# Load order, holds, banks and blank products at the start of a retention and ELU kernel

## The chip, the cores and the metric

The kernel runs on one core of a Trainium2 chip. The metric is the device time of one execution in microseconds (us), of which several runs are made and the median is given. A separate execution is recorded by the hardware profiler, and all lines of profile in this document come from such executions. The engines are TensorE (PE: matrix products, PEld: loading of their stationary operand), VectorE (DVE), ScalarE (ACT), GpSimd (POOL) and SyncE (SP), which here issues every transfer between HBM and SBUF.

## The reference

A retention layer (a linear attention with a decaying state, per head) is followed by a feed-forward layer with an ELU. All values are fp32.

```python
B, H, S, D = 4, 8, 768, 64                       # q, k, v: (B, H, S, D)
gamma = 1.0 - 2.0 ** (-5.0 - np.arange(H))
for t in range(S):
    state = gamma * state + k[:, :, t] (outer) v[:, :, t]
    y[:, :, t] = q[:, :, t] @ state / np.sqrt(D)
x = y.transpose(0, 2, 1, 3).reshape(3072, 512)
h = x @ w_in                                      # 512 x 2048
g = np.where(h > 0.0, h, np.exp(np.minimum(h, 0.0)) - 1.0)
out = g @ w_out                                   # 2048 x 512
```

## The kernel before

The 3072 tokens are handled in six blocks of 512 tokens, and a block in four chunks of 128. For each chunk two tiles of 0.5 MB are loaded: `qk` (q and k, transposed) and `kvn` (k and v). The retention of a chunk is computed in 64-token halves. `score_products` makes the scores (L276, 64x64 products into `sc`), `mask_pair` or `scores` masks them on VectorE (L297, L287), `scale_v` multiplies v by the decay (L250, or L247 on ACT for chunk 3), `state_products` and `state_sum` make the states (L307; L317, L319), and `outputs` makes the outputs `y` from scores (L341) and from states (L367), with a tiny copy `seen` (L355) between two groups of accumulations. At its end `outputs` multiplies `y` by the decay table `etab` into the block's input `xb` (L376). Before the first output exists, tables are set up: positions by POOL, `etab` by four exponentials on ACT (L209), `vf` for the scaling of v, and the mask `cmask`.

The weights arrive as 16 pieces of 1 MB of float64 bits (`wraw`, through a ring of three `stage` buffers). A piece is turned into fp32 by two steps on ACT (`prepare`, L142 and L144) and four on VectorE (`decode`, L165, L168, L171, L174); when a piece has been decoded, the next one is loaded into its buffer. Pieces 0 to 7 are `w_a` and `w_b` (from `w_in`), pieces 8 to 15 become `w_s` (from `w_out`).

The first block is computed plainly: `plain_first` (L443 for the first five tiles of hidden units, in two token halves, then L454) and `plain_second` (L468). While it runs, combinations of the weights are made by VectorE (`combine_w_out`, L509; `combine_w_in`, L536) and stored to scratch memory. From the second block on the products use Strassen's scheme: `first` (L602), later `first_twice` and `second_twice` (L772, L811), which fetch the stored combinations (`wq`).

The order of the instructions on each engine is the order in which the program writes them; no scheduler changes it. At the start `prepare(2)` and `take(4)` decode the first half of piece 0, and then chunks 0 and 1 are worked through. `take()` advances the decoding of the current piece by one VectorE step. The loads stand in front of everything:

```python
    load_piece()
    load(0)
    load(1)
    load_piece()
    load(2)
    load(3)
    load_piece()
```

PSUM is divided into a ring of four banks (`ps_r`: scores, states, outputs and some hidden tiles) and four fixed banks: `a` (two buffers), `b` and `d`.

Of the kernel before, what the change touches and what calls it, by code (L numbers as in the profile page):

```python
# [9 lines left out]
FP32 = mybir.dt.float32  # L10
# [7 lines left out]
def kernel(  # L18
# [32 lines left out]
    nc = tc.nc  # L51
# [45 lines left out]
    def load(m):  # L97

        if m >= NCHUNK:
            return  # L100
        qk = ldpool.tile([P, 2, HP, C], FP32, name="qk", tag="qk")
        nc.sync.dma_start(qk.rearrange("p a h c -> p (a h c)"), qkv[m, :, 0:1024])
        kv = ldpool.tile([C, 2, H, D], FP32, name="kvn", tag="kvn")
        nc.sync.dma_start(kv.rearrange("p a h c -> p (a h c)"), qkv[m, :, 1024:2048])
        raw[m] = (qk, kv)

# [4 lines left out]
    NPIECE = 2 * NQ + NF  # L113
    staged, prepared, decoded = [], [], []

    def load_piece():
        n = len(staged)
        if n < NPIECE:

            t = stage.tile([P, 1024, 2], U32, name="wraw", tag="stage")  # L120
            nc.sync.dma_start(t.rearrange("p c w -> p (c w)"), w_bits[n].bitcast(U32))
            staged.append(t)

# [57 lines left out]
        for _ in decode():  # L181
            pass

    load_piece()
    load(0)
    load(1)
    load_piece()
    load(2)
    load(3)
    load_piece()  # L190


    pos_t = t4.tile([P, S], I32, name="pos_t", tag="t4")
    nc.gpsimd.iota(pos_t, pattern=[[1, S]], base=0, channel_multiplier=0)


    head = lambda a, u, c: 2 * (2 * u + c) + a
# [1 line left out]
    for a in range(2):  # L199
        for u in range(2):  # L200
            for c in range(2):
                nc.vector.memset(lny[c * D : (c + 1) * D, a, u : u + 1], math.log(gammas[head(a, u, c)]))

    post = t4.tile([P, S], FP32, name="post", tag="t4")
    nc.vector.tensor_copy(post, pos_t)
    etab = const.tile([P, 2, 2, S], FP32, name="etab")
    for a in range(2):
        for u in range(2):
            nc.scalar.activation(etab[:, a, u, :], post, AF.Exp, scale=lny[:, a, u : u + 1])  # L209
    pos_s = const.tile([P, NCH, H], I32, name="pos_s")  # L210
    nc.gpsimd.iota(pos_s, pattern=[[C, NCH], [0, H]], base=0, channel_multiplier=1)
    lng = const.tile([P, H], FP32, name="lng")
    for h in range(H):
        nc.vector.memset(lng[:, h : h + 1], math.log(gammas[h]))
# [13 lines left out]
    for sub in range(2):  # L228
        r = slice(sub * D, (sub + 1) * D)
        nc.vector.tensor_copy(cmask[r, :], causal[r, r])  # L230

    xb = const.tile([P, 4, TB], FP32, name="xb")
# [5 lines left out]
    def scale_v(m):  # L240
        if m >= NCHUNK:
            return
        i = chunks[m][1]
        qk, kv = raw[m]
        if m == 3:
            for h in range(H):
                nc.scalar.activation(kv[:, 1, h, :], kv[:, 1, h, :], AF.Copy, scale=vf[:, i, h : h + 1])  # L247
            return
        eng = nc.vector if m == 0 else nc.gpsimd
        eng.tensor_tensor(  # L250
            out=kv[:, 1], in0=kv[:, 1], in1=vf[:, i].unsqueeze(2).to_broadcast([C, H, D]), op=ALU.mult
        )
# [76 lines left out]

    def outputs(tb, pp, first=False):  # L330

        y = [ps_r.tile([P, 2 * 2, 2, D], FP32, name="y", tag="r") for _ in range(2)]
        for x in range(2):
            kv = raw[tb * CPB + 2 * pp + x][1]
            for j in range(4):
                a, u = divmod(j, 2)
                pt = raw[tb * CPB + 2 * pp + (x if first else a)][0][:, 1].rearrange("p h c -> p (h c)")
                for sub in range(2):
                    for c in range(2):
                        p = 2 * u + c  # L340
                        nc.tensor.matmul(  # L341
                            y[sub][rows(c), j, x, :], lhsT=kv[rows(sub), 1, head(a, u, c), :],
                            rhs=pt[rows(sub), ((a if first else x) * HP + p) * D :][:, 0:D],
                            start=(x == 0 and j == 0), stop=False, skip_group_check=True,
                        )
            if first and x == 0:
                yield
        for other in range(2):
            if not other:
                yield  # L350
            else:

                for sub in range(2):
                    seen = epool.tile([P, 8], FP32, name="seen", tag="seen")
                    nc.vector.tensor_copy(seen.rearrange("p (j x) -> p j x", x=2), y[sub][:, :, :, 0])  # L355
                yield
            for x in range(2):
                q = raw[tb * CPB + 2 * pp + x][0]
                for u in range(2):
                    for a in range(2):  # L360
                        sub = a ^ other
                        n = 4 * pp + 2 * x + sub
                        if fresh(tb, n):
                            continue
                        for c in range(2):
                            p = 2 * u + c
                            nc.tensor.matmul(  # L367
                                y[sub][rows(c), 2 * a + u, x, :], lhsT=state(tb, n)[rows(a), p, :],
                                rhs=q[rows(a), 0, p, rows(sub)], start=False, stop=True, skip_group_check=True,
                            )  # L370
        if first:
            yield
        i = chunks[tb * CPB + 2 * pp][1]
        for sub in range(2):
            place = lambda t: t.rearrange("p j (x s c) -> p j x s c", x=2, s=2)[:, :, :, sub, :]
            nc.vector.tensor_tensor(  # L376
                out=place(xb[:, :, 2 * pp * C : 2 * (pp + 1) * C]), in0=y[sub],
                in1=place(etab.rearrange("p a u t -> p (a u) t")[:, :, i * C : (i + 2) * C]), op=ALU.mult,
            )
# [81 lines left out]
    def plain_second():  # L461

        ops = [bank(x).rearrange("p a b -> p (a b)") for x in "aabd"]
        for n, f in enumerate(ORDER_F):
            wo = decoded[2 * NQ + n]
            for row in range(2):
                for d in range(4):
                    nc.tensor.matmul(  # L468
                        ops[d], lhsT=wo[:, row, (d if row else d ^ 2) * P :][:, 0:P], rhs=g_plain[row * NF + f],
                        start=(n == 0 and row == 0), stop=(n == NF - 1 and row == 1),  # L470
                    )
            so = t4.tile([P, 4, 256], FP32, name="so", tag="t4")
            tt = lambda o, x, y, op: nc.vector.tensor_tensor(out=o, in0=x, in1=y, op=op)
            a21, a11, a12, a22 = (wo[:, r, 256 * d : 256 * d + 256] for r in range(2) for d in range(2))
            tt(so[:, 0], a21, a22, ALU.add)
            tt(so[:, 1], so[:, 0], a11, ALU.subtract)
            tt(so[:, 2], a11, a21, ALU.subtract)
            tt(so[:, 3], a12, so[:, 1], ALU.subtract)
            nc.sync.dma_start(quarters(f)[:, 8:16], so.rearrange("p a (d c) -> p (a d) c", c=P))
            if n < 5:  # L480
                send_small()
            sources = wo.rearrange("p r (d c) -> p (r d) c", d=2)[:, 1:4], so
            if n % 2:
                last = combine_w_out(n // 2, low, sources)

                for _ in itertools.islice(last, 8 if n < NF - 1 else 4):
                    pass
            low = sources
            if n >= 5:
                send_small()  # L490
            held["last"] = last if n % 2 else None
            yield
        for d in range(4):
            ot = gq["T3"][:, 2 * d : 2 * d + 2, :]
            eng = (nc.scalar.copy, nc.vector.tensor_copy)[d % 2]
            eng(ot.rearrange("p a b -> p (a b)"), ops[d])
            nc.sync.dma_start(out[0, d // 2, :, :, d % 2, :].rearrange("t p c -> p t c"), ot)
# [453 lines left out]
    def take(count=1):  # L951
        for _ in range(count):
            next(piece, None)

    prepare(2)
    piece = decode(True)
    take(4)
    sc = [ps_r.tile([P, 2, HP, D], FP32, name="sc", tag="r") for _ in range(2)]
    score_products(sc, 0, 0, 0)
    scale_v(0)  # L960
    scale_v(1)
    mask_pair(sc, 0)
    kvs = [ps_r.tile([P, 2, HP, D], FP32, name="kv", tag="r") for _ in range(2)]
    state_products(kvs, 0, 0, 0, range(2))
    score_products(sc, 0, 0, 1)
    state_sum(kvs, 0, 0, 0, 0)
    state_sum(kvs, 0, 0, 0, 1)
    mask_pair(sc, 1)
    take(2)
    prepare()  # L970
    y = outputs(0, 0, True)
    next(y)
    state_products(kvs, 0, 0, 1, [0])
    next(y)
    state_sum(kvs, 0, 0, 1, 0)
    take()

    next(y)
    next(y)
    state_products(kvs, 0, 0, 1, [1])  # L980
    take(2)
    next(y, None)
    state_sum(kvs, 0, 0, 1, 1)
    scale_v(2)
    decode_all()
# [251 lines left out]
```

## Time and profile before

| | |
|---|---|
| runs before | 646.38, 647.08, 647.72, 648.02 us; median 647.39 us |
| profiled execution | 646.38 us, of which the recorded span is 644.6 us |
| TensorE busy | 629.8 us, 98% of the span |
| VectorE busy | 496.5 us, 77% |
| ACT busy | 240.4 us, 37% |
| POOL busy | 39.3 us, 6% |
| moved by transfers | 139.72 MB, 217 GB/s on average |
| first product on TensorE | 7.50 us after the span's start |
| first product of `plain_first` | 19.03 us |

A row of a timeline gives the start, the length, the engine, the line, the operation and its tiles. A row of the chain of waits gives the start, the length and the work that the end was waiting for at that time. An entry of the waits reads: engine, line and tile, what it waited for, the sum in us, how many times, and the longest. Transfers are listed by line with their size and the time from issue to landing.

### The profile page before, as it was taken

The numbers are of one execution on the slowest core, as the hardware profiler recorded it, in microseconds if no ns is written. First come the engines' busy times: TensorE is split into PE (matmuls) and PEld (weight loads), VectorE is DVE, ScalarE is ACT, GpSimd is POOL, SyncE is SP. The second block draws the span as 40 slices with busy tenths as digits, with TensorE's granted clock in tenths as the row PEclk, the third lists the DMA queues.
The fourth block names the chain that finished last, engine by engine and source line by source line (L and its number), as shares of the span: only waits on it lengthen the run. The fifth ranks groups of instructions, "written<-read, shape, count | busy, mean of one in ns | idle before, by whom it ended". The sixth has DMA issues, their size and how long they took to land.

```text
span 644.6 us, 15861 instructions
## 1 busy us (share of the span) xinstructions
PE 629.8 (98%) x6512; PEld 542.6 (84%) x6512; DVE 496.5 (77%) x887; ACT 240.4 (37%) x463; POOL 39.3 (6%) x38
## 2 busy tenths in 40 slices
PE   4999999999999999999999999999999999999998
PEld 3774444548889999989999989999988999988997
DVE  5789789998979776589777488867569959557976
ACT  6477641204552112546112465211464311356311
POOL 1001100000460000100000110000020000000000
DMA  8638989999387789802799811688840688710694
GB/s 340 250 133 317 326 234 257 285 277 284 113 282 263 235 260 314 271 11 71 234 299 295 299 66 34 207 282 269 292 178 3 197 261 261 238 44 1 213 313 162
DMA packets 85209, 139.72 MB, mean 217 GB/s; under 512 B 6672, under 2 KB 38800, under 8 KB 82832
## 3 DMA queue, kind: packets, MB, share of 16 engines
q1 hardware_dynamic: 85136, 138.70, 66.3%
q8 instruction: 52, 0.85, 0.5%
q14 instruction: 21, 0.17, 0.1%
HBM read 114.56 MB, written 24.12 MB: 215 GB/s over the span
## 4 chain that ended last, share of the span: by engine, by line
PE 92%; DVE 3%; POOL 2%; DMA 1%; issue 1%; ACT 1%; SPq 0%; POOLq 0%
PE pa L811 20%; PE pa L772 10%; PE pd L811 9%; PE hp L454 6%; PE pb L811 5%; PE pa L726 4%; PE pa L468 4%; PE pb L772 4%; PE qa L772 3%; PE y L341 2%; PE pd L726 2%; PE qd L772 2%; PE pd L772 2%; PE pb L468 2%; PE pd L468 2%; PE y L367 2%
## 5 line engine op out<-in xcount | busy, mean ns | idle before, releaser
L819 ACT COPY ms<-pa 128x128 f32<-128x128 f32 x104 | 27.6, 265 | 146.6 <-PE pa L811 145.0
L811 PE MATMUL pa<-ts,wq 128*128 128x128 f32 x560 | 74.1, 275 | 0.3 <-ACT ms L819 0.3
L811 PE MATMUL pd<-ts,wq 128*128 128x128 f32 x552 | 73.2, 275 | 0.0
L811 PEld LDWEIGHTS pa<-ts,wq 128*128 128x128 f32 x560 | 68.5, 192 | 0.8 <-ACT ms L819 0.5
L811 PEld LDWEIGHTS pd<-ts,wq 128*128 128x128 f32 x552 | 67.1, 192 | 0.3 <-DVE res L823 0.2
L811 PE MATMUL pa<-gC,wq 128*128 128x128 f32 x480 | 65.0, 278 | 0.7 <-issue 0.7
L422 ACT ACTIVATE r<-r 128x512 f32<-128x512 f32 x96 | 60.5, 630 | 3.0
L811 PEld LDWEIGHTS pa<-gC,wq 128*128 128x128 f32 x480 | 59.1, 192 | 2.3 <-issue 0.9
L421 ACT ACTIVATE r<-gC 128x512 f32<-128x512 f32 x64 | 39.9, 624 | 33.4 <-DVE gC L780 33.4
L823 DVE TENSOR_TENSOR res<-pd,ms 128x128 f32<-128x128 f32 x68 | 19.5, 287 | 36.8 <-PE pd L811 35.6
L250 POOL TENSOR_TENSOR kvn<-kvn,vf 128x512 f32<-128x512 f32 x22 | 25.4, 1159 | 348.4 <-DMA kvn<-in_qkv_dram 234.4
L425 DVE SCALAR_TENSOR_TENSOR gC<-r,gC 128x512 f32<-128x512 f32 x64 | 43.4, 711 | 0.7 <-ACT r L422 0.7
L688 DVE TENSOR_TENSOR ts<-gC,ts 128x512 f32<-128x512 f32 x60 | 41.3, 688 | 1.0
L688 DVE TENSOR_TENSOR ts<-gC 128x512 f32<-128x512 f32 x60 | 41.0, 684 | 0.0
L811 PE MATMUL pb<-gC,wq 128*128 128x128 f32 x240 | 32.8, 277 | 0.1
L468 PE MATMUL pa<-gC,w_s 128*128 128x512 f32 x64 | 30.6, 600 | 0.0
L811 PEld LDWEIGHTS pb<-gC,wq 128*128 128x128 f32 x240 | 29.5, 192 | 0.8 <-DVE gC L425 0.8
L844 ACT COPY res<-pa 128x128 f32<-128x128 f32 x34 | 9.0, 265 | 56.5 <-PE pa L811 56.5
L780 DVE TENSOR_TENSOR gC<-qa,gC 128x512 f32<-128x512 f32 x8 | 5.5, 692 | 25.1 <-PE qa L772 18.3
L552 ACT COPY m<-pa 128x512 f32<-128x512 f32 x24 | 13.9, 579 | 24.6 <-PE pa L772 13.2
L772 PE MATMUL pa<-xt,w_s 128*128 128x256 f32 x96 | 23.0, 382 | 0.0
L772 PE MATMUL pa<-xt,w_b 128*128 128x256 f32 x96 | 23.0, 382 | 0.0
(206 smaller groups left out, 1229.3 us busy)
## 6 DMA issues: line engine op xcount, KB each, us to landing
wq<-scratch_dram SPq DMA_DIRECT2D x277, 256.0 KB, 4.6
wraw<-in_w_dram SPq DMA_DIRECT2D x16, 1024.0 KB, 5.9
qk<-in_qkv_dram SPq DMA_DIRECT2D x24, 512.0 KB, 6.9
kvn<-in_qkv_dram SPq DMA_DIRECT2D x24, 512.0 KB, 7.9
scratch_dram<-w_s SPq DMA_DIRECT2D x8, 512.0 KB, 7.2
scratch_dram<-so SPq DMA_DIRECT2D x8, 512.0 KB, 5.7
out_dram<-res SPq DMA_DIRECT2D x14, 256.0 KB, 4.4
scratch_dram<-gT SPq DMA_DIRECT2D x12, 256.0 KB, 3.7
```

The lines of the kernel that those rows point to most:

```text
L250: eng.tensor_tensor(out=kv[:, 1], in0=kv[:, 1], in1=vf[:, i].unsqueeze(2).to_broadcast([C, H, D]), op=ALU.mult)
L421: nc.scalar.activation(e, h, AF.Relu, scale=-1.0)
L422: nc.scalar.activation(e, e, AF.Exp, scale=-1.0)
L425: nc.vector.scalar_tensor_tensor(g, e, -1.0, h, ALU.add, ALU.max)
L454: nc.tensor.matmul(hp, lhsT=w[n][:, fi, j // 2, j % 2, :], rhs=xb[:, j, :], start=(j == 0), stop=(j == 3))
L468: nc.tensor.matmul(ops[d], lhsT=wo[:, row, (d if row else d ^ 2) * P :][:, 0:P], rhs=g_plain[row * NF + f], start=(n == 0 and row == 0), s ...
L688: sub = lambda o, x, y: nc.vector.tensor_tensor(out=o, in0=x, in1=y, op=ALU.subtract)
L726: nc.tensor.matmul(ps[:, f, :], lhsT=lhs[f], rhs=xs[j][k], start=(begin and f == 0), stop=True, skip_group_check=True,)
L772: nc.tensor.matmul(ps[:, fi, :], lhsT=w[:, fi, j2, :], rhs=x[:, j2, :], start=(j in (1, 7) and fi == 0 and j2 == 0), stop=(j2 == 1), skip_ ...
L811: nc.tensor.matmul(ps, lhsT=w[:, f, :], rhs=ts[j][k][:, f, :], start=(begin and f == 0), stop=(f == 3), skip_group_check=True,)
L819: nc.scalar.copy(m, ps)
L823: nc.vector.tensor_tensor(out=o, in0=x, in1=y, op=ALU.add)
```

## The change

- Loads: the first chunk is loaded ahead of the first piece of weights. Loads after that can be held: `hold` copies, on POOL, one element of another tile into the tile to be loaded, so that the load is issued only when that other tile has landed. qk 1 is held behind qk 0, kv 1 behind kv 0, piece 1 behind piece 0, qk 2 behind kv 1, qk 3, kv 2 and kv 3 behind piece 1, piece 2 behind kv 2.
- Tables: the large position table and `etab` are made after `vf` and `cmask`.
- First outputs: those of chunks 0 and 1 are written to banks `b` and `d` instead of the ring.
- Blank products: nine products of zeros (two of 512 columns, seven of 256) are written to bank `a`, in five places; nothing reads them.
- Order: chunk 0 is worked through before piece 0 is prepared; the decoding steps and chunk 1 follow. v of chunk 1 is scaled on VectorE instead of POOL.
- The last `combine_w_out`: two of its steps are done in `plain_second` instead of four; the others run beside `first(0)`.

```diff
+        for which in range(2):
+            load_one(m, which)
+
+    def load_one(m, which, behind=None):
+        if which == 0:
+            raw[m] = [ldpool.tile([P, 2, HP, C], FP32, name="qk", tag="qk"), None]
+            t = raw[m][0].rearrange("p a h c -> p (a h c)")
+        else:
+            raw[m][1] = ldpool.tile([C, 2, H, D], FP32, name="kvn", tag="kvn")
+            t = raw[m][1].rearrange("p a h c -> p (a h c)")
+        hold(t, behind)
+        nc.sync.dma_start(t, qkv[m, :, 1024 * which : 1024 * which + 1024])
+
+    def hold(t, other):
+        if other is not None:
+            nc.gpsimd.tensor_copy(t[0:1, 0:1], other[0:1, 0:1])
...
-    def load_piece():
+    def load_piece(behind=None):
...
+            hold(t[:, :, 0].bitcast(FP32), behind)
...
+    blank = hpool.tile([P, TB], FP32, name="blank", tag="h")
+    nc.vector.memset(blank, 0.0)
...
+    load(0)
+    load_piece()
+    for which in range(2):
+        load_one(1, which, raw[0][which][:, 0, 0])
+    pieces = lambda n: staged[n][:, :, 0].bitcast(FP32)
+    load_piece(pieces(0))
+    load_one(2, 0, raw[1][1][:, 0, 0])
+    for m, which in ((3, 0), (2, 1), (3, 1)):
+        load_one(m, which, pieces(1))
+    load_piece(raw[2][1][:, 0, 0])
...
-        eng = nc.vector if m == 0 else nc.gpsimd
+        eng = nc.vector if m < 2 else nc.gpsimd
...
-        y = [ps_r.tile([P, 2 * 2, 2, D], FP32, name="y", tag="r") for _ in range(2)]
+        if first:
+            y = [bank(x).rearrange("p a (b x d) -> p (a b) x d", b=2, x=2) for x in "bd"]
+        else:
+            y = [ps_r.tile([P, 2 * 2, 2, D], FP32, name="y", tag="r") for _ in range(2)]
...
-                for _ in itertools.islice(last, 8 if n < NF - 1 else 4):
+                for _ in itertools.islice(last, 8 if n < NF - 1 else 2):
...
+    warm = bank("a").rearrange("p a b -> p (a b)")
+
+    def unread(count, n):
+        for _ in range(count):
+            nc.tensor.matmul(warm[:, 0:n], lhsT=blank[:, 0:P], rhs=blank[:, 0:n], start=True, stop=True, skip_group_check=True)
+
+    unread(2, TB)
+    sc = [ps_r.tile([P, 2, HP, D], FP32, name="sc", tag="r") for _ in range(2)]
+    score_products(sc, 0, 0, 0)
+    mask_pair(sc, 0)
+    scale_v(0)
+    unread(1, TH)
+    kvs = [ps_r.tile([P, 2, HP, D], FP32, name="kv", tag="r") for _ in range(2)]
+    state_products(kvs, 0, 0, 0, range(2))
+    state_sum(kvs, 0, 0, 0, 0)
+    state_sum(kvs, 0, 0, 0, 1)
     prepare(2)
     piece = decode(True)
-    take(4)
...
     y = outputs(0, 0, True)
     next(y)
+    unread(2, TH)
+    score_products(sc, 0, 0, 1)
+    take(2)
+    mask_pair(sc, 1)
+    scale_v(1)
+    unread(3, TH)
+    take()
     state_products(kvs, 0, 0, 1, [0])
     next(y)
     state_sum(kvs, 0, 0, 1, 0)
+    prepare()
     take()

     next(y)
+    take(2)
     next(y)
     state_products(kvs, 0, 0, 1, [1])
+    unread(1, TH)
+    next(y, None)
     take(2)
-    next(y, None)
     state_sum(kvs, 0, 0, 1, 1)
```

More of the change, by code (lines that the diff above doesn't have):

```diff
@@ L100, in load @@
             return
[L101 to L105, printed above, removed]
+        for which in range(2):
[12 more added lines that the diff above has]
+            nc.gpsimd.tensor_copy(t[0:1, 0:1], other[0:1, 0:1])
     w_a_, w_b_ = (const.tile([P, NQ, 2, 2, 2, P], FP32, name=x) for x in ("w_a", "w_b"))
@@ L182, in decode_all @@
             pass
[L184 to L194, printed above, removed]
+    blank = hpool.tile([P, TB], FP32, name="blank", tag="h")
+    nc.vector.memset(blank, 0.0)
     head = lambda a, u, c: 2 * (2 * u + c) + a
@@ L202 @@
                 nc.vector.memset(lny[c * D : (c + 1) * D, a, u : u + 1], math.log(gammas[head(a, u, c)]))
[L204 to L209, printed above, removed]
     pos_s = const.tile([P, NCH, H], I32, name="pos_s")
     nc.gpsimd.iota(pos_s, pattern=[[C, NCH], [0, H]], base=0, channel_multiplier=1)
+    pos_t = t4.tile([P, S], I32, name="pos_t", tag="t4")
+    nc.gpsimd.iota(pos_t, pattern=[[1, S]], base=0, channel_multiplier=0)
     lng = const.tile([P, H], FP32, name="lng")
@@ L230 @@
         nc.vector.tensor_copy(cmask[r, :], causal[r, r])
+    post = t4.tile([P, S], FP32, name="post", tag="t4")
+    nc.vector.tensor_copy(post, pos_t)
+    etab = const.tile([P, 2, 2, S], FP32, name="etab")
+    for a in range(2):
+        for u in range(2):
+            nc.scalar.activation(etab[:, a, u, :], post, AF.Exp, scale=lny[:, a, u : u + 1])
+    load(0)
[8 more added lines that the diff above has]
+    load_piece(raw[2][1][:, 0, 0])
     xb = const.tile([P, 4, TB], FP32, name="xb")
@@ L953, in take @@
             next(piece, None)
+    warm = bank("a").rearrange("p a b -> p (a b)")
[12 more added lines that the diff above has]
+    state_sum(kvs, 0, 0, 0, 1)
     prepare(2)
     piece = decode(True)
-    take(4)
[L958 to L970, printed above, removed]
     y = outputs(0, 0, True)
     next(y)
+    unread(2, TH)
[5 more added lines that the diff above has]
+    take()
     state_products(kvs, 0, 0, 1, [0])
```

## The prediction

> **What bounds the kernel now.** I read the page's busy shares first, then its slices, the waits of TensorE, the chain of waits over the first 45 us, and the DMA issues one by one.
>
> ```profile
> PE 629.8 (98%) x6512; PEld 542.6 (84%) x6512; DVE 496.5 (77%) x887; ACT 240.4 (37%) x463; POOL 39.3 (6%) x38
> ...
> PE   4999999999999999999999999999999999999998
> ```
>
> The matmul row is full in every slice but the first (16.1 us each). Whatever this change gives must come from that slice, or be a later hole that it makes.
>
> ```profile
> PE sc L276 <- DMA qk<-in_qkv_dram: 7.5, 1, 7.5
> PE kv L307 <- DVE kvn L250: 1.4, 1, 1.4
> ...
> PE pa L443 <- DVE xb L376: 0.7, 1, 0.7
> ```
>
> TensorE's own waits over the whole run: 7.5 us for the first chunk, then small ones for VectorE. After 19.03 us it waits for 1.3 us in all. So the end is the time of the first full-size product (L443), plus what holds the products up before the steady stretch:
>
> ```profile
> 9.30 0.69 DVE kvn L250
> ...
> 12.55 1.34 PE y L341 x30
> ...
> 18.29 0.69 DVE xb L376
> ...
> 19.03 5.35 PE pa L443 x16
> 24.37 1.09 PE sc L276 x64
> ...
> 32.63 1.92 PE hp L443 x8
> 34.55 3.45 PE pa L443 x16
> ```
>
> (Chain of waits: start, length, what.) The same 16 passes cost 5.35 us at 19 us and 3.45 us at 34 us: 1.90 us are lost to a slow start. (An fp32 product leaves two passes.) The granted clock reads 1.00 throughout, so the loss is visible only in the pass rate, here of line L443 and then of TensorE as a whole:
>
> ```profile
> 21.00:22.00 1.00, 1.00 (x4) 0.81 (x3) 1.00 0.96 393
> ...
> 23.00:24.00 1.00, 1.00 (x7) 0.87 (x5) 1.00 0.18 74
> ```
> ```profile
> 14.00:16.00 2.00, 2.00 (x71) 1.00 1.02 404
> ```
>
> Start, length, matmul busy (count). About 0.43 us a pass until 22.4 us, 0.216 us after: full rate came 3.4 us after 19.03. The second fence shows TensorE busy all of 14 to 16 us with 64x64 products, which did not raise the rate.
>
> ```profile
> wraw<-in_w_dram SPq DMA_DIRECT2D x1, 1024.0 KB, 4.9
> qk<-in_qkv_dram SPq DMA_DIRECT2D x1, 512.0 KB, 6.3
> kvn<-in_qkv_dram SPq DMA_DIRECT2D x1, 512.0 KB, 7.1
> ...
> kvn<-in_qkv_dram SPq DMA_DIRECT2D x1, 512.0 KB, 8.5
> ```
>
> Single issues: piece 0 at 0.73 us, qk 0 at 1.17, kv 0 at 1.64, kv 1 at 2.82. They landed at 5.6, 7.45, 8.75 and 11.3 us: in the order issued, 0.5 MB per 1.3 us, the engines full. Likewise kv 3 landed at 20.4 and piece 2 at 22.9. Issued into an empty queue (36.33 us), a megabyte takes 4.8 us.
>
> **The change part by part.** Chunk 0 (1 MB) goes in front of piece 0 (1 MB), so the two exchange places: qk 0 at about 4.3 us (5.6 less 1.3), kv 0 at 5.6, piece 0 at 8.75. Chunk 1 still has the same 2 MB before it: 10.0 and 11.3 us, no gain.
>
> *Holds.* Eight POOL copies of one element each wait for a landing, and SP issues behind them in order. One copy lies between 0.10 us (the 128x1 memset row) and 0.21 us (the smallest IOTA); I take 0.10, plus 0.33 us for the issue. Holds for qk 1, kv 1 and piece 1 cost nothing, since 1 MB or more is still in the queue when they are issued; without that cover each would cost up to 2.2 us of empty engines (4.8 less 2.6 us of transfer). Piece 1: released at 8.75, lands at 13.85 (13.8 before). qk 3, kv 2 and kv 3 wait for it: issued from 14.1, they land at about 17.6, 18.8 and 20.1. Piece 2 waits for kv 2: 18.8 + 0.25 + 4.8 = 23.9 us, 1.0 us later than before. On POOL, the scaling of chunk 2 (1.04 us) is queued behind the last hold; that hold waits for kv 2, which the scaling needs anyway. Piece 3 is issued by SP behind piece 2, lands near 26.7 us, and is first read (38.2 us before) with over 7 us to spare.
>
> *First outputs in banks b and d.* Chunk 0's outputs no longer need the ring's score buffers back, so they run at once. No instruction is added.
>
> *VectorE's order to the first xb.* Chunk 0's scaling, masks and state sum now come before decoding, under the wait for piece 0. ACT decodes it from 8.75: 0.64 + 0.65 us, 10.05. From there VectorE runs without a gap: two decode steps 0.43 + 0.43, mask 0.75, scaling of kv 1 0.68 (moved here from POOL, where it took 1.04), third step 0.69, state sum 0.42, fourth 0.69, seen 0.35, two steps 0.86, xb 1.29: sum 6.6, so first L443 at about 16.8 us, against 19.03. This holds if TensorE's pieces fit between: scores of chunk 1 by 10.95, kv products and outputs after 12.45, last outputs by 15.45. At full rate they do (0.55 us per 32 passes against 1.1 at half rate).
>
> *Nine blank products.* Two of 512 columns and seven of 256: 8 and 14 passes of 256-column size, 22 x 0.427 = 9.4 us at half rate or 4.7 at full rate. The first two start when the blank is set (between 0.09 us, a small memset, and 0.69, a 128x512 operation; I take 0.5, so 1.3 us) and end at 4.7, when qk 0 has just come: hidden. The rest lie in waits for VectorE or for a landing at full rate. At half rate they would not fit (first rival).
>
> Here the Trainium skill ("TensorE: Matmul & The Clock Gate", Part 1, the HAM clock gate) is to be weighed. The rows: 3.4 us from 19.03 to full rate, and no rise over 10 to 18 us of nearly gapless 64x64 work. The page says that the clock doubles after about 3.4 us of activity in a free-running window, and drops after an idle one. Its window length agrees; taken as plain busyness it would have raised the clock by 16 us, and the trace says it did not. By the page, small products keep the clock up once raised: the 1.90 us go. By the rows, small products hardly count, and between 11.9 and 16.8 us there are only 0.43 us of blanks: the clock may have dropped again at 16.8, and the 1.90 us stay (second rival). I take the first, since over 24 to 33 us a mix with many small products lost no rate. The page's free-running window also makes the loss of before vary by up to 1.7 us more (half of 3.4); the runs spread over 1.64 us.
>
> *What is late next.* With both gains L443's 16 passes end at 16.8 + 3.45 = 20.25. Scores of chunks 2 and 3 (1.09) follow. Chunk 3 is scaled on ACT for 2.02 us from 20.1: kv products wait about 0.45 us, which had 3 us of cover before. Products pb and pd then start at 22.75; VectorE has w_b ready at 22.5. The half decode of piece 2 (23.9 + 1.35 on ACT, then VectorE behind masks and sums) ends near 27.9, and "seen", queued behind it, near 28.15, so the last outputs wait some 0.6 us, 0.3 more than before. hp (L443) starts at 28.9 against 32.63: 3.7 us gained.
>
> A second rule, from "DMA: Bandwidth & Descriptors" (the fit in "Anatomy of one DMA", given there for the gpsimd path): 2.0 us plus bytes at 436 GB/s, 4.4 us for a piece; the row has 4.8. Over the three held links the rule would land piece 2 at 22.7 and give 0.3 us more. I keep the row.
>
> *Last small weights moved back.* Two VectorE steps of 0.69 us leave the end of L468's stage for the next one, and their four stores go behind the output stores and a chunk load on SP; the store is fetched only from 187 us, 30 us later. It brings xt 1.3 us forward: at 148.48 the first xt product started 0.1 us late. Gain 0.1 us. The next stage has VectorE gaps of 1.25, 0.76 and 0.64 us at 154 to 161 us to take the two steps; uncovered they would cost 1.4.
>
> Everything behind 29 us (decoding, ELU, stores) is paced by TensorE, VectorE or freed buffers, not by fixed times, so it shifts as a whole. Sum: 646.38 - 3.7 - 0.1 = 642.6 against the profiled execution (span 644.6, 1.8 us around it), which is the fastest of four; the median is 647.39. If the clock's start is no longer left to chance the new median lies near its own profile; I forecast 643.0.
>
> **The rivals.**
> *Blanks at half rate (slower).* If the first 3.4 us of blanks do not raise the clock, those before chunk 1's scores end at 11.4 instead of 9.5, the three behind them at 15.1, then kv products and outputs at half rate, and xb ends at 19.9. The slow L443 follows as before: 0.9 us worse than the profiled run, plus up to 1.7 us if the window falls badly; 648.2 in the middle. It decides when TensorE is still at 0.43 us a pass at 8.6 us. For it: blanks of 3.4 us seldom fill a free-running 3.4 us window. Against: scores and another blank follow at once, to 6.75.
> *Clock raised, then lost.* L443 at about 17.0 but slow: 2.0 us gained, the later waits covered: 644.3, or 645.2 with a mean phase.
> *Holds run the queue dry.* If each hold costs 1 us more than I count, chunk 1 and pieces 1 and 2 land 1 to 3 us later: gain 1 us or so, 645.5.
> *Nothing gained:* chunk 1 lands when it did, so loads alone move little. If VectorE's order gains nothing and the clock stays slow, 647.
>
> **How the numbers follow.** All parts work 0.54 (641.8 to 643.8), clock lost 0.17, holds dry 0.09, nothing gained 0.07, half rate 0.13. A measurement of this kernel can tell about 0.2%, 1.3 us, so faster is below 646.1: the first three less their upper tails, 0.74; same, those tails, the fourth and the lower part of the half-rate case, 0.13; slower, the rest of it and holes not seen here, 0.13. Range 641.6 to 647.8.
>
> **What would show it.** Right: the first L443 product near 16.8 us with 16 passes in about 3.5 us; hp near 28.9; qk 0 landed near 4.3 and kv 1 near 11.3; later waits of TensorE under 1.5 us. Wrong: 0.43 us passes at 17 us; scores of chunk 1 behind blanks that end after 10.5; DMA idle between 11 and 20 us; or a new TensorE wait behind 30 us.

## The result and the profile after

The changed kernel takes 649.55 us (median of 43 runs, 646.79 to 652.48) against 647.47 us for the kernel before (64 runs): a ratio of 1.0036, 95% interval 1.0026 to 1.0046. It is slower by 2.3 us, where 643.0 us was forecast. Its profiled execution took 648.74 us (span 647.0), 2.36 us more than that of before.

The busy times, and the slices of TensorE and of its granted clock:

```profile
PE 635.3 (98%) x6530; PEld 543.8 (84%) x6530; DVE 496.6 (77%) x889; ACT 240.7 (37%) x463; POOL 40.2 (6%) x45
...
PE   7999999999999999999999999999999999999998
...
PEclk9899999999999999999999999999999999999999
```

The first slice rose from 4 to 7, which is the work with blanks and earlier chunks. The clock row is new: the second slice (from 16.2 us) shows 8, a clock that was raised and then fell. TensorE is busy 5.5 us longer in all, since it now computes blanks too.

TensorE's own waits (what waited, for what; sum in us, times, longest):

```profile
PE y L390 <- issue: 1.5, 1, 1.5
PE pd L390 <- issue: 1.5, 1, 1.5
PE pa L982 <- DVE blank L200: 1.5, 1, 1.5
PE sc L295 <- DMA qk<-in_qkv_dram: 0.9, 1, 0.9
PE kv L326 <- DVE kvn L269: 0.8, 1, 0.8
PE y L390 <- DVE seen L378: 0.6, 1, 0.6
PE pa L625 <- DVE xt L418: 0.6, 1, 0.6
```

The wait of 7.5 us for the first chunk is gone: blanks run from 1.46 us, and the first scores follow them at 5.16 us, in 0.69 us where before took 1.13:

```profile
7.50 1.13 PE L276 MATMUL sc<-qk 64*64 64x64 f32 x32 [7.50 <-DMA qk<-in_qkv_dram]
```
```profile
5.16 0.69 PE L295 MATMUL sc<-qk 64*64 64x64 f32 x32
```

(The first of these fences is before, the second after.) Two waits of 1.5 us "for issue" are new: TensorE stood with nothing to wait for that the profile shows. The timeline (start, length, engine, line, tiles, idle time before) has the first of them, and what follows:

```profile
16.65 0.27 PE L390 MATMUL pd<-qk,kvn 64*64 64x64 f32 x1 [1.52 <-issue]
...
18.71 5.38 PE L466 MATMUL pa<-xb,w_a 128*128 128x256 f32 x16 [0.47 <-DVE xb L399]
...
23.25 0.87 POOL L117 COPY wraw<-kvn 1x1 f32<-1x1 f32 x1 [6.58 <-DMA kvn<-in_qkv_dram]
24.02 1.16 PE L295 MATMUL sc<-qk 64*64 64x64 f32 x64
24.09 1.03 POOL L269 TENSOR_TENSOR kvn<-kvn,vf 128x512 f32<-128x512 f32 x1
24.41 2.02 ACT L266 ACTIVATE kvn<-kvn,vf 128x64 f32<-128x64 f32 x8 [5.87 <-DMA kvn<-in_qkv_dram]
25.17 1.65 PE L326 MATMUL kv<-kvn 64*64 64x64 f32 x64
...
33.62 1.99 PE L466 MATMUL hp<-xb,w_a 128*128 128x256 f32 x8
```

The first L466 product (L443 before) is at 18.71 us, 0.3 us earlier than before and 1.9 later than forecast. Its 16 passes take 5.38 us, as slowly as before, and the scores of chunks 2 and 3 behind them end at 25.18 us. The scaling of chunk 2 on POOL starts at 24.09, behind the copy of the last hold, and ends at 25.12; that of chunk 3 on ACT starts at 24.41. The state products start at 25.17. So here the late start and the late loads end within 0.1 us of each other, TensorE shows no wait for a scaling, and this profile alone can't say which of the two counts; the experiments can. hp is at 33.62, against 32.56 before and 28.9 in the forecast. What POOL and ACT waited for are the loads, here single issues with the time from issue to landing:

```profile
wraw<-in_w_dram SPq DMA_DIRECT2D x1, 1024.0 KB, 6.9
qk<-in_qkv_dram SPq DMA_DIRECT2D x1, 512.0 KB, 5.5
qk<-in_qkv_dram SPq DMA_DIRECT2D x1, 512.0 KB, 4.2
kvn<-in_qkv_dram SPq DMA_DIRECT2D x1, 512.0 KB, 6.2
kvn<-in_qkv_dram SPq DMA_DIRECT2D x1, 512.0 KB, 7.0
wraw<-in_w_dram SPq DMA_DIRECT2D x1, 1024.0 KB, 4.8
```

These are piece 1 (issued at 9.27 us, landed at 16.14), qk 2 (11.87, 17.39), qk 3 (16.46, 20.61), kv 2 (16.90, 23.13), kv 3 (17.36, 24.39) and piece 2 (24.15, 28.95). The busy share of the DMA engines from 8 to 30 us, in 40 slices of 0.55 us, with the total below it:

```profile
DMA  9999958999597211068987898971000969899999
...
DMA packets 1222, 5.94 MB, mean 270 GB/s; under 512 B 131, under 2 KB 131, under 8 KB 870
```

There are two holes, at 14.6 to 17.3 us (qk 3, kv 2 and kv 3 held behind piece 1) and at 22.9 to 25.0 us (piece 2 held behind kv 2). Before moved 7.39 MB in the same 22 us.

Set against before pass by pass, the profiled execution adds up as follows: hp 1.05 us later; 0.64 us more at 150 us, the wait for xt; 0.16 us by 180 us; 1.52 us by the second stand, at 219 us; then 1.01 us back at 414 us, where before stood and this kernel does not. The sum is 2.36. The stand of before:

```profile
414.21 0.49 PE L811 MATMUL pa<-gC,wq 128*128 128x128 f32 x2 [0.75 <-issue]
```

One execution shows one fall of the clock. Each run also lists its mean granted clock, and a fall of 3.41 us to one half is 0.0026 of the span. By this count 39 of the 44 executions of the changed kernel on record, the profiled one among them, had at least one fall (0.997 or less) and 12 had two or more; the other five took 646.79 to 647.85 us.

### The profile page after: what moved, and what is told of

The parts are those of the page before. It is cut to its first block, busy times and chain, and to the rows that moved or that the text cites. A ratio compares the mean times of both kernels' runs of the same rounds, so it can differ in the third digit from the quotient of the medians.

```text
span 647.0 us, 15914 instructions
## 1 busy us (share of the span) xinstructions
PE 635.3 (98%) x6530; PEld 543.8 (84%) x6530; DVE 496.6 (77%) x889; ACT 240.7 (37%) x463; POOL 40.2 (6%) x45
## 4 chain that ended last, share of the span: by engine, by line
PE 69%; DVE 7%; DMA 2%; POOL 1%; issue 1%; SPq 1%; ACT 1%; POOLq 0%; DVEq 0%
PE pa L834 20%; PE pa L795 10%; PE pd L834 9%; PE pb L834 5%; PE pa L749 4%; PE pb L795 4%; PE qa L795 3%; PE pd L749 2%; PE qd L795 2%; PE pd L795 2%; POOL wi L700 1%; PE y L364 1%; PE y L390 1%; PE sc L295 1%; PE kv L326 1%
## 5 line engine op out<-in xcount | busy, mean ns | idle before, releaser
L575 ACT COPY m<-pa 128x512 f32<-128x512 f32 x24 | 13.9, 580 | 25.4 <-PE pa L795 14.2
```

What stands on the lines that cost most here:

```text
L575: nc.scalar.copy(m, ps)
```

## The experiments

All were timed beside the kernel before on the same chip. "Start" is the first L466 product (L443 in the kernel before) with the length of its 16 passes, and hp its first product in that tile; both are of one profiled execution. The last column is the ratio times 647.4 us, less 647.4.

| kernel | start, us | hp, us | median, us | ratio to before (95%) | us |
|---|---|---|---|---|---|
| before | 19.03, 5.35 | 32.56 | 647.2 to 647.7 | | |
| after | 18.71, 5.38 | 33.62 | 649.55 | 1.0036 (1.0026 to 1.0046) | +2.3 |
| e1 no holds | 19.17, 4.01 | 31.55 | 645.41 | 0.9969 (0.9947 to 0.9990) | -2.0 |
| e2 no blanks | 18.53, 5.21 | 33.57 | 648.03 | 1.0010 (0.9994 to 1.0026) | +0.6 |
| e3 neither | 19.46, 5.22 | 33.85 | 648.01 | 1.0007 (0.9994 to 1.0020) | +0.5 |
| e4 small weights as before | 16.78, 3.69 | 33.20 | 651.26 | 1.0054 (1.0037 to 1.0072) | +3.5 |
| e5 first three holds | 17.01, 3.69 | 29.97 | 646.20 | 0.9991 (0.9978 to 1.0005) | -0.6 |
| e6 first two holds | 16.73, 3.69 | 29.10 | 644.60 | 0.9969 (0.9953 to 0.9985) | -2.0 |
| e7 later five holds | 17.52, 3.69 | 34.99 | 649.47 | 1.0037 (1.0018 to 1.0056) | +2.4 |
| e8 before with blanks | 19.15, 3.72 | 31.87 | 646.16 | 0.9993 (0.9979 to 1.0006) | -0.5 |
| e9 e6, 48 records more | 17.80, 3.69 | 30.04 | 646.60 | 0.9982 (0.9969 to 0.9995) | -1.2 |
| e10 e6, 96 records more | 18.66, 4.03 | 31.05 | 647.42 | 0.9997 (0.9979 to 1.0015) | -0.2 |
| e11 e6, small weights as before | 17.48, 3.69 | 29.95 | 646.31 | 0.9981 (0.9968 to 0.9994) | -1.2 |
| e12 e6, no blanks | 19.04, 6.20 | 33.43 | 648.82 | 1.0024 (1.0007 to 1.0041) | +1.6 |

**e1: no holds**

```diff
     def hold(t, other):
-        if other is not None:
+        if False:
```

> The changed kernel with its eight holds taken out; every load is issued as soon as SP reaches it, in the same order. Theory H (the holds make the later loads late, and these set the start of hp): kv 3 lands near 20.4 us instead of 24.4, piece 2 near 23 instead of 29, the wait for seen before the last outputs falls from 0.6 to under 0.3 us, and hp starts at about 32.3 us or earlier, against 33.6 in the changed kernel and 32.6 before: some 1.3 us faster than the changed kernel. Rival P (the wait of TensorE near 15 us and the half-rate passes from 18.7 us set it): TensorE still stands for about 1.5 us near 15 us, the first L466 product still starts near 18.7 us at half rate, and the time is within 0.5 us of the changed kernel. Rival D (that wait comes of the transfer queue's state, which the holds made): the wait near 15 us goes too, first L466 near 17 us, some 3 us faster than the changed kernel.

Without holds piece 1 landed at 15.0 us, kv 3 at 20.10 and piece 2 at 22.85, all earlier than in the changed kernel by 1.1 to 6.1 us; chunk 1 alone came later (kv 1 at 12.51 against 11.55). The eight holds cost 4.3 us together. (The interval of e1, with nine executions, is some 1.4 us to either side.) TensorE waited 1.9 us for chunk 1 (9.4 to 11.3 us), and its clock read 0.50 from 11.6 to 15.1 us, so not all of the raised clock was used.

**e2: no blanks, and e3: no holds and no blanks**

```diff
-    unread(2, TB)
...
-    unread(1, TH)
...
```

> The changed kernel without its nine blank products. Theory I (TensorE stood at 15.1 us because it had used up the instructions fetched so far: the small products at full rate use them twice as fast, and the blanks add 36 instruction records before that point): at half rate and 36 records later TensorE meets the same place after 16 us or in a wait that is there anyway, so the stand near 15 us is gone or under 0.5 us. First L466 then near 17 to 18 us, but at half rate for 3.4 us; hp still near 33.6 us, since the late piece 2 sets it. Rival S (the stand is not tied to the number of instructions): a stand of about 1.5 us still near 15 us. On either, the time is within 1 us of the changed kernel if the holds set the start of hp.

> Neither holds nor blanks; the order, the banks, the tables and the small weights stay as changed. If holds and the stand of TensorE are the two costs and the new order is worth its 2 us, the first L466 product starts near 17 us at half rate, hp near 30.5 us, and the time is about 2 us below before. If the order is worth nothing by itself, the first L466 product starts near 19 us and the time is that of before.

What is left in e3 (order, banks, tables, small weights) is within 0.2% of before: the start is at 19.46 and slow. With no holds the blanks are worth 2.5 us (e3 to e1). With all holds they cost 1.7 us (e2 to after): hp is at 33.57 and 33.62, so nothing that they gain gets past the late loads, and what they do later (e9, e10) stays. That they also give the clock a height to fall from is in the runs: no execution of e2 or e3 has a mean clock below 0.999.

**e4: four steps of the last small weights as before**

```diff
-                for _ in itertools.islice(last, 8 if n < NF - 1 else 2):
+                for _ in itertools.islice(last, 8 if n < NF - 1 else 4):
```

> The changed kernel with four steps of the last combination in the first block instead of two, as before. Theory W (moving two steps away cannot be what made the xt wait of 0.55 us at 150 us; that came of VectorE waiting 2.0 us for a store at 126 us, so without the move xt would be 1.3 us later still): the xt wait is the same or larger, up to 1.9 us, if VectorE is as late again, and 0.1 us if it is not; the time is 0 to 1.3 us longer than the changed kernel. Rival: the move itself costs (its four stores, or the two steps in the next stage), and the time is 0.5 us or more shorter.

In its profiled execution the stand at 15 us did not occur, and the start is the forecast one to 0.02 us. Yet hp is at 33.20, since the next wait is the loads':

```profile
16.78 3.69 PE L466 MATMUL pa<-xb,w_a 128*128 128x256 f32 x16 [0.48 <-DVE xb L399]
```
```profile
PE kv L326 <- POOL kvn L269: 2.0, 1, 2.0
```

kv 2 had landed at 22.24 us. Behind this wait the clock read 0.50 from 24.6 to 28.0 us. So hp is late without the stand too: the late loads are enough, by a wait and by the fall of the clock behind it. The median of e4 is 2.95 us above its profiled execution, whose clock fell once. Of its 17 executions eight had two or three falls (mean clock 0.995 and 0.992, 651.26 to 655.49 us), and only one had none (647.72). This tells why its trace is faster than its runs; what makes it 1.2 us slower than the changed kernel is not in the trace, and e11 asks the same question where the loads are early.

**e5: holds on qk 1, kv 1 and piece 1; e6: on qk 1 and kv 1; e7: on the later five alone**

```diff
     for which in range(2):
         load_one(1, which, raw[0][which][:, 0, 0])
-    load_piece(pieces(0))
-    load_one(2, 0, raw[1][1][:, 0, 0])
+    load_piece()
+    load_one(2, 0)
     for m, which in ((3, 0), (2, 1), (3, 1)):
-        load_one(m, which, pieces(1))
-    load_piece(raw[2][1][:, 0, 0])
+        load_one(m, which)
+    load_piece()
```

(e6; e5 keeps `pieces(0)`, e7 keeps the later ones and takes the two of chunk 1 and that of piece 1 away.)

> The changed kernel with holds on qk 1, kv 1 and piece 1 alone; qk 2 and all loads after it are issued without waiting. Theory A (the later five holds empty the queue, the first three cost nothing): kv 1 at about 11.6 us, kv 3 at 20 to 21 and piece 2 at 23, as before, in place of 24.4 and 29.0; first L466 near 17 with 16 passes in 3.5 to 4 us, hp near 29 to 30; 643.5 to 645. Theory B (every hold costs, the first three too): kv 1 at 11.6 but piece 1 at 16 again, kv 3 past 22, hp near 32, 647. Theory C (loads are not it; the stand of TensorE without a wait at 15 us and the clock's fall behind it are): the stand of 1.5 us comes again, 16 passes in over 5 us, 648.

> The changed kernel with holds on qk 1 and kv 1 alone; piece 1 and all behind it are issued at once. Theory A: as with three holds or 0.3 us better, kv 1 at 11.6, piece 1 at 14, kv 3 at 19.5, 643 to 645. Theory B: two holds still cost, kv 1 lands no earlier than without holds (12.5) or piece 1 later than 15; 646. Theory C: a stand near 15 us and slow passes, 648.

> The changed kernel with the five later holds alone (qk 2, qk 3, kv 2, kv 3, piece 2); chunk 1 and piece 1 are issued at once. Theory A: all of the cost is here: kv 1 at 12.5 and piece 1 at 15.0 as without holds, then kv 3 at 22.5 to 24 and piece 2 at 27 to 29, a wait for chunk 3 or for the scaling of chunk 2, seen late; 648 to 650. Theory B: half of the cost or less, 646.5 to 647.5. Theory C: no relation to the loads; the time follows whether a stand without a wait falls in the first 25 us.

In e6 the start and hp come within 0.2 us of the forecast:

```profile
16.73 3.69 PE L466 MATMUL pa<-xb,w_a 128*128 128x256 f32 x16 [0.48 <-DVE xb L399]
...
29.10 2.00 PE L466 MATMUL hp<-xb,w_a 128*128 128x256 f32 x8
```

and its DMA engines from 8 to 30 us show no hole before 22.8 us:

```profile
DMA  9899999989999999999899999995688998522000
...
DMA packets 1424, 7.32 MB, mean 333 GB/s; under 512 B 163, under 2 KB 163, under 8 KB 906
```

In e7, with the later five alone, the tile kvn from 20 to 26 us reads (copies and operations with mean length and start):

```profile
L117 POOL COPY wraw<-kvn x1: 173/173/173, 24.0 to 24.0; 1x1 f32<-1x1 f32 x1
L269 POOL TENSOR_TENSOR kvn<-kvn,vf x1: 1031/1031/1031, 24.1 to 24.1; 128x512 f32<-128x512 f32 x1
...
  POOL kvn L269: 6.0, 2
who waited for it (us, times):
  PEld kv L326: 3.1, 1
  PE kv L326: 2.9, 1
```

kv 2 landed at 23.88, the hold copy of piece 2 took 0.17 us, the scaling 1.03, and the state products started at 25.23 after 2.9 us of waiting; the clock then read 0.50 from 26.5 to 29.9 us, and hp is at 34.99. So the cost lies in the later five: 4.4 us alone (e1 to e7), 2.9 us on top of the first three (e5 to after). The first two show no cost (e1 and e6 both -2.0) and bring chunk 1 forward by 0.9 us in e6 (kv 1 at 11.62; in e11, with the same holds, by 0.1). Piece 1's hold, with qk 1 and kv 1 (1 MB) still queued at its issue, costs 1.4 us by the middle values (e6 to e5; the intervals overlap): it was issued at 9.10 in place of 6.88 and landed at 15.88 in place of 15.06. In e7, without this hold, it landed as late, at 15.89, so the landing alone does not prove the cost. Theory A is right on the later five, and for piece 1 the runs speak against it.

The profiled execution of e6, 646.57 us, is 1.97 us above its median: it is one of 4 in 22 whose clock fell. The other 18 have a median of 644.41 us. In the kernels with blanks and the later holds (changed, e4, e7) 63 of 70 executions had a fall, in those with blanks and without these holds or added records (e1, e5, e6, e11) 21 of 75. So part of the holds' price is most likely the clock that falls behind the waits, as it did in the traces of e4 and e7.

**e8: the kernel before with blanks alone**

```diff
+    unread(3, TB)
     prepare(2)
     piece = decode(True)
     take(4)
...
+    unread(1, TH)
     state_products(kvs, 0, 0, 0, range(2))
     score_products(sc, 0, 0, 1)
+    unread(2, TH)
...
     state_products(kvs, 0, 0, 1, [1])
+    unread(1, TH)
```

> The kernel before with blank products alone: three of 512 columns ahead of the first scores, one of 256 ahead of chunk 0's states, two behind chunk 1's scores, one ahead of the last chunk-1 work. Loads, order and banks as before. If the raised clock by itself is worth its 1.9 us: scores of chunk 0 in 0.7 us, the 16 passes of L443 in 3.5 us, hp at 30.7, 645.5. If the clock is lost again in the waits of TensorE (7.5 us for chunk 0, 1.4 for the scaling): passes in about 5.3 us, 647.5. If the blanks lie in the way of chunk 0 and 1 at half rate: 648.5.

The passes fell to 3.72 us, but hp to 31.87 only (0.7 us earlier, not 1.9), and the time is not separable from before's. The clock read 0.50 from 10.5 to 13.9 us, after a wait of 1.8 us for the scaling, so part of the chunk work was slow again. A stand of 0.6 us (up to 30.2 us) and one of 1.5 us (up to 218.2 us) are new.

**e9, e10: where TensorE stands**

```diff
     scale_v(0)
     unread(1, TH)
+    for _ in range(12):     # e10: 24
+        nc.tensor.matmul(warm[0:D, 0:D], lhsT=blank[0:D, 0:D], rhs=blank[0:D, 0:D], start=True, stop=True, skip_group_check=True)
```

> The changed kernel with holds on qk 1 and kv 1 alone, plus twelve blank 64x64 products (48 records on TensorE: 24 weight loads, 24 passes) in the wait of 0.8 us for chunk 0's scaling, where they take 0.45 us. The start should be as without them (first L466 at 16.7, hp at 29.1). Theory A: TensorE stands where its instructions have not come yet, at every 256th record, if the records just before it went fast. Record 4033 then falls 48 records earlier into the burst of 64x64 products at 213 us, with about 130 fast records before it in place of 180; the stand of 1.8 us inside L390 shrinks to 0.4 us or goes, but the stand near 529 us may stay, as another burst moves in front of its boundary (record 11457); median 643.0 to 644.0 against 644.6. Theory B: the stand belongs to the place in the program (its transfers, its banks): it stays in L390 at the same product, 644.6 to 645.

> As with 48 records, with 24 such products (96 records, 0.9 us at full rate, of which about 0.1 is not covered by the wait). Theory A: record 4033 has about 75 fast records before it: no stand above 0.3 us in L364 or L390 at 213 us; record 11457 has about 130 in its burst; another boundary may be hit instead (record 3777, whose burst now ends just before it, near 206 us). Median 643 to 644.5. Theory B: the stand of 1.8 us stays at the same product of L390; 644.7 to 645.2.

In the profiled execution of e6 TensorE stood inside L390, as in the changed kernel, and what follows shows the price (second fence: stretch in us; the last three columns are granted clock, DMA share and GB/s):

```profile
216.34 0.44 PE L390 MATMUL y<-qk,kvn 64*64 64x64 f32 x10 [1.84 <-issue]
```
```profile
217.00:218.00 1.00, 1.00 (x9) 1.00 (x9) 0.00 (x0) 0.00 (x0) 0.00 (x0) 0.75 0.15 57
218.00:219.00 1.00, 1.00 (x7) 1.00 (x7) 0.00 (x0) 0.27 (x1) 0.00 (x0) 0.50 0.00 0
...
221.00:222.00 1.00, 1.00 (x11) 1.00 (x10) 0.00 (x0) 0.27 (x1) 0.00 (x0) 1.00 0.47 123
```

1.84 us of standing, and then some 3.4 us at half clock, which cost 1.6 us more: e6 was 3.04 us ahead of before at 209 us and 0.41 us behind at 221 us. With 48 records more, in e9, that stand is gone, and one of 2.54 us is found in the burst of state products before it:

```profile
210.38 0.45 PE L326 MATMUL kv<-kvn 64*64 64x64 f32 x7 [2.54 <-issue]
```

Counted in order of start (weight loads, passes and TensorE's semaphore instructions), the stand of e6 comes after 4033 records and that of e9 after 3777; e10 stands after 3777 too, and after 3521. All stands for issue of over 0.6 us in the profiled executions of this case come after 449, 961, 3521, 3777, 4033, 4545, 8641 or 11457 records, and all of these are 193 more than a multiple of 256. Theory A holds: the place is set by the count, not by the program. The expected times were missed: the stand moved to another burst rather than going away, and the start was 1.1 and 1.9 us later, because the extra products ran before the clock had risen (scores of chunk 0 in 1.14 and 1.13 us, then 23 passes in 1.60 us in e9, where 0.45 was counted for all).

**e11: e6 with four steps of the small weights**

> The changed kernel with holds on qk 1 and kv 1 alone, and four steps of the last small weights in the stage of L491 as before, not two. If the move is worth the 0.1 us of the wait for xt in the profile of before: within 0.3 us of 644.6, xt wait 0.3 to 0.5 us. If it is worth the 1.3 us by which it brings xt forward: 645.9, with a wait for xt of over 1 us at 145 us. If it costs (its steps late in the stage behind, its stores late): 644.

The wait for xt grew from 0.2 to 1.1 us:

```profile
PE pa L625 <- DVE xt L418: 1.1, 1, 1.1
```

The time is 0.8 us above e6's, which fits; that hp was 0.85 us later too, after a longer wait for chunk 1 (1.4 in place of 0.5 us), makes it an upper bound for the move.

**e12: e6 without blanks**

> The changed kernel with holds on qk 1 and kv 1 alone and without the nine blank products. Theory A (the blanks raise the clock early, but their 36 records also move record 4033 into the end of a burst of 64x64 products at 213 us): the first L466 comes 1.5 to 2 us later than with blanks (18.2 to 18.7) and its 16 passes take 5.2 us, hp at about 32.3 in place of 29.1; the stand of over 1 us inside L390 at 213 to 217 us is gone or under 0.5; so of the 3.2 us lost at the start some 1.5 to 2 come back there: median 645.8 to 646.5. Theory B (the alignment of the records is small change): the whole 3.2 us show, 647.5 to 648. Theory C (with the loads right the blanks do nothing): 644.6, hp at 29 to 30.

hp is at 33.43, 4.3 us later than with blanks, and the time 3.6 us higher: theory B. Theory A's return did not come, since without the 36 records of the blanks TensorE stands elsewhere: 1.1 us from one record to the next at 219 us (record 4033, now behind its burst) and 1.2 us at 414 us (record 8641).

## Why the prediction was wrong

- **Chunk 0 first:** right. qk 0 landed at 4.75 us (4.3 forecast), kv 0 at 6.40 (5.6), piece 0 at 9.02 (8.75), kv 1 at 11.55 (11.3).
- **"Holds for qk 1, kv 1 and piece 1 cost nothing":** for the first two no cost shows. Piece 1 landed at 16.14 us in place of 13.85. Over all traces with chunk 0 in front it landed at 14.5 to 15.9 us without its hold (eight traces, mean 15.1) and at 15.9 to 16.3 with it (four, mean 16.1). So about 0.9 us is the hold's: 1 MB in the queue was not cover enough. The other 1.3 us the sum had too little without any hold.
- **The later holds:** this is the step that failed. qk 3 was put at 17.6, kv 2 at 18.8, kv 3 at 20.1 and piece 2 at 23.9 us; they came at 20.61, 23.13, 24.39 and 28.95. Link by link, 2.3 us was piece 1's lateness handed on; qk 3 took 4.2 us from its issue where the sum had 3.5; kv 2 landed 2.5 us behind it where the sum had 1.2, as the emptied queue did not take up its old rate at once; and piece 2 was issued 1.0 us after kv 2's landing where the sum had 0.25, since here the copy of its hold took 0.87 us (0.17 in e4 and e7). It is the named rival "holds run the queue dry"; its mechanism was right, and its price, 1 us per hold and 645.5 us in all, too small. Measured, the six holds beyond chunk 1's cost 4.3 us (e6 to after).
- **The start at 16.8 us with full-rate passes, hp at 28.9:** the sum over VectorE was right, as e6 shows (16.73; 3.69; 29.10), but the profiled execution does not reach it. Its start was late by a stand of 1.52 us at 15.1 us that no step had. Behind that stand the clock read 0.50 from 18.8 to 22.2 us: the second rival, "clock raised, then lost", came true there. e4, which escaped the stand, still had hp at 33.20, and taking the later holds away brings the time below before (e1 and e6; e5's -0.6 is not clear of it). So the loads bind with or without the stand; what the stand would cost with early loads was not run.
- **Blanks raise the clock:** right. The first scores took 0.69 us in place of 1.13. The rival that was to end on the slower side, blanks at half rate, shows for the first few us in some executions (scores in 0.99 to 1.14 us in e4 to e7, e9 and e10), but the start was on time in those of e4 to e6; the slower result came by the loads, for which only a milder case had been allowed. That the clock's start would no longer be left to chance was wrong: it rose at 4.8 to 7.5 us, as the last section shows.
- **The clock rule weighed there** (the Trainium skill, "TensorE: Matmul & The Clock Gate", Part 1, a fall after an idle window of about 3.4 us): the rows here are harder. 1.5 to 1.9 us without products, at 15 us in the changed kernel, at 9.4 us in e1 and at 214.5 us in e6, were followed by half clock for 3.41 us. That the window is 3.4 us long and free-running agrees; that it must be wholly idle does not: about half is enough (last section). Nor does every such gap count: 1.55 us at 219 us in the changed kernel, and even 2.54 us at 208 us in e9, left the clock full, as each lay across two windows.
- **"Everything behind 29 us shifts as a whole":** wrong in two ways. The wait for xt took 0.6 us here and 1.1 us in e11, so the move of the small weights, costed at 0.1 us, is worth up to 0.8 us once the start is early. And the 36 records of the blanks moved TensorE's stands: before loses 0.75 us at 414 us, this kernel 1.55 us at 219 us. In its profiled execution e6 was 3.46 us ahead of before at hp and lost 3.45 us between 209 and 221 us, so that its time there equals that of before; its median, 2.0 us below before, shows that most executions lose less.

What stays open: why e4 is slower than the changed kernel; why chunk 1 lands later when it is not held (kv 1 at 12.4 to 12.5 us in e1, e3 and e7, at 11.4 to 12.4 when held); and what sets the moment at which TensorE's instructions are fetched, and with it each stand, since a trace shows one execution. What e6 would take without any stand was not tried. e6 is the fastest version found; e1 equals it within its wider interval, though its hp is 2.45 us later.

## What to carry to other kernels

A hold that waits for a landing pays an empty queue, unless more is queued behind the held transfer's predecessor than the queue takes to restart; sum a chain of holds link by link with the latency of an idle queue (here 3.7 to 4.2 us for qk 3's 0.5 MB and 4.8 to 5.0 for piece 2's 1 MB), and hand each link's lateness on to the next. When the start of a kernel is brought forward, look for what downstream was just in time (xt here, 0.1 us late), because it takes the gain. Count a wait of TensorE behind a raised clock twice, once for itself and once for the fall that can follow, and look at the mean clock of all runs before taking one trace for the kernel. When many small products are added or removed, expect stands without a wait to move, and compare traces by the count of instructions at which they occur before giving the loss to the change.

## What the runs showed of the hardware

- TensorE runs out of instructions. The queue for instructions moved 52 packets of 16 KB in an execution, in the changed kernel for 13,322 records of TensorE (its semaphore instructions counted too), one for every 256:

```profile
q8 instruction: 52, 0.85, 0.5%
```

  Most of the stands come behind bursts of 64x64 products (about 130 records per us). In the packet records of the traces each of the 23 such stands (0.6 to 2.5 us of idle TensorE) ends 2.2 to 2.6 us after such a packet began, or 3.2 us in the one case where the packet took 1.93 us and not 0.9 to 1.1. (Two of them, after 8641 records in e2 and e12, the profile puts down to VectorE.) The Trainium skill ("Runtime: NRT & Kernel Launch", Instruction fetch mechanics) has the blocks of 256 and calls the crossing mostly hidden; at most blocks it cost nothing here either, once with 254 records in the 2 us before (e5, at 287 us), but the 23 stands had 67 to 214. So the pace alone does not decide; by these figures the packet had begun too late.
- Such a stand can cost twice: 1.84 us and then 1.6 us by the fallen clock (e6).
- The clock changes on a grid of 3.4133 us that runs through an execution. In the six traces with two falls these lie 184, 185, 182, 125, 182 and 186 steps apart (changed, e1, e4, e6, e7, e8), whole to 0.001. With the clock up, the six steps before the falls in mid-run had 1.75 to 2.12 us without products (changed 1.75, e6 1.84, e1 1.90, e4 2.02, e8 2.09, e7 2.12), and no step of these traces or of e5, e9 and e11 with 1.57 us or less (e5) was followed by one. The stand at 219 us in the changed kernel left 0.78 and 0.76 us in two steps, that of 2.54 us in e9 1.08 and 1.47.
- So the moment at which the blanks raise the clock is not set by the kernel. It rose at the end of the first step that products filled to all but 0.13 us or less: at 4.82 us in e1, 5.13 in the changed kernel, 5.69 in e11, 5.87, 5.93 and 6.04 in e6, e5 and e7, 7.07 in e8, 7.52 and 7.55 in e9 and e4. A first step with 0.73 to 1.20 us idle (e4, e9, e8) was not enough. The first scores, behind the same two large blanks, took 0.69 us in e1 and the changed kernel, 0.90 in e11, 0.99 to 1.07 in e6, e5 and e7, and 1.13 to 1.14 in e4 and e9. Without blanks it rose at 21.6 to 24.1 us (e2, e3, e12), at the end of a step of full-size passes; in e12 the step from 13.9 to 17.3 us, of 64x64 products alone with 0.27 us idle, had not raised it. Before its first rise a trace has no record of the clock and reads 1.00.
